# Second half of a weight load cut in two, and the last store handed to two queues, in a fused attention + gated-MLP kernel

## The chip, the core and the metric

The kernel runs on one core of a Trainium2 chip. A core has a matrix engine (TensorE, PE in the profile; its weight loads are listed as PEld), a vector engine (VectorE, DVE), a scalar engine (ScalarE, ACT), GpSimd (POOL) and SyncE (SP), which here only issues DMAs. Each engine runs its own list of instructions in order; they wait for one another through counters (semaphores). The metric is device time of the whole program in microseconds, the median of several runs; lower is better. The profiler also records one execution in full: its span runs from the first to the last recorded instruction.

## What is computed

The input is one sequence of 2048 tokens with 512 features. With LN for a layer norm without scale and bias, cut to what matters:

```python
xn = LN(A_x)                                  # 2048 x 512
# A: 32 heads of 16, each token looks at 8 keys, 2 tokens apart, backwards
q, k, v = split(xn @ A_wqkv)
a = softmax(q . k[s - 2w], w = 0..7) ; A = (sum_w a_w v[s - 2w]) @ A_wo
# B: gated MLP with mixing over tokens
z = gelu(xn @ B_w_in)                         # 2048 x 1376, halves z1 and z2
g = B_w_sp @ LN(z2) + B_b_sp                  # mixes over tokens
B = (z1 * g) @ B_w_out
out = A_x + A + B                             # 2048 x 512, bfloat16
```

## The kernel before

The 2048 tokens are 16 tiles of 128 tokens (`P`). The order of the work is written out by hand: every engine runs its instructions in the order in which the program names them, so moving a line moves the work in that engine's list.

The start is what the first edit touches. SP issues the loads in this order: tile 0 of x, tile 1 of x (lines 180 and 181), tiles 2 and 3 together (182), then the z2 half of `B_w_in` into `w_z2` (lines 183 and 184), then the next four tiles of x (`load_x`, line 176), the two weights for q and k (188) and two more loads of x. `w_z2` holds 128 partitions by 4 row blocks (`kc` = 0 to 3, 128 of the 512 features each) by 688 columns. Before, it comes in two loads of two row blocks each. VectorE takes the layer-norm statistics of a tile (`ln_stats`), ScalarE the square root (`roots`), VectorE the reciprocal and the normalized tile `xn` (`ln_apply`). For the first four tiles PE transposes `xn` in four blocks into a PSUM tile `pt` (`transpose_pe`, line 224), and ScalarE (tiles 0 and 1, line 226) or VectorE (tiles 2 and 3, line 228) copies it into `xnT`. Before the first real work PE runs small matmuls on a tile of ones (`spin`, line 102).

`z2_part(i, pz, kc)` (line 239) is the product of tile i with row block kc: two matmuls of 344 columns each (line 241), accumulated in PSUM over the four values of kc. `z2_gelu` (line 245) is ScalarE's gelu of the finished tile. Lines 439 to 452 interleave tiles 0 and 1: block 0 and 1 of both, then blocks 2 and 3 of tile 0 with its gelu, then the transposes of tile 2, then blocks 2 and 3 of tile 1 with its gelu, then the transposes of tile 3, then `z2_tile(2)` and `z2_tile(3)` whole.

In between lie the products for q, k and v, the sliding attention on VectorE, the mixing over tokens (line 576, the largest single part of PE's work), z1 (588) and the output products (747 and 756). These are not touched.

The end is what the second edit touches. `out_b` and `store` (lines 742 and 760) finish one tile of 128 tokens after another: six matmuls, one add on VectorE, and one store of 128 KB from SP (764). The very last tile is finished by `last_tile` (line 722) in two halves of 256 columns: six matmuls (729), an add on VectorE (731) and a store of 64 KB (732), both stores issued from SP. After that the program ends (the records at line 809): SP waits until every completion counter has its count, and all engines meet.

Each DMA adds 16 to a completion counter when it has landed. The trace shows eight such counters (numbers 100, 102, 104, 105, 106, 107, 109, 110), which the DMAs of SP and ACT take in turn in program order, so that a DMA waits for the one that used its counter eight DMAs earlier. GpSimd's DMAs have counters of their own (111 to 115).

Of the kernel before, what the change touches and what calls it, by code (L numbers as in the profile page):

```python
# [13 lines left out]
P = 128  # L14
# [16 lines left out]
F = 1376  # L31
FH = 688
# [15 lines left out]
def kernel(  # L48
# [17 lines left out]
    A = nc.scalar  # L66
    G = nc.gpsimd
    PE = nc.tensor
    SP = nc.sync

    x2 = A_x.rearrange("b s d -> (b s) d")
    out2 = out.rearrange("b s d -> (b s) d")
# [14 lines left out]
    def bank_pair(name, two=False):  # L87
        turn[0] += 1
        pool = ps_b if turn[0] % 3 == 0 and not two else ps_a
        return pool.tile([P, 2, 512], F32, name=name, tag="mm")  # L90
# [66 lines left out]
    w_z2 = e1.tile([P, C, FH], BF16, name="w_z2")  # L157
# [11 lines left out]
    w_in_r = B_w_in.rearrange("(k p) f -> p k f", p=P)  # L169
# [10 lines left out]
    SP.dma_start(x0[:, 0, :], x2[0:P, :])  # L180
    SP.dma_start(x0[:, 1, :], x2[P:2 * P, :])
    SP.dma_start(x0[:, 2:4, :], x2[2 * P:4 * P, :].rearrange("(i p) d -> p i d", p=P))  # L182
    for k0 in (0, 2):
        SP.dma_start(w_z2[:, k0:k0 + 2, :], w_in_r[:, k0:k0 + 2, FH:F])
    xq.append(x0)
    load_x(1)
    for s in range(2):
# [12 lines left out]
    def ln_apply(i):  # L200
        xn = xnp.tile([P, D], BF16, name="xn")
        V.tensor_scalar(xn[:], xq[i // 4][:, i % 4, :], mv[:, i, 0:1], rstd[:, i:i + 1], ALU.subtract, ALU.mult)
        return xn
# [17 lines left out]
    def transpose_pe(i, xn):  # L221
        pt = ps_aux.tile([P, C, P], BF16, name="pt", tag="aux")
        for c in range(C):
            PE.transpose(pt[:, c, :], xn[:, c * P:(c + 1) * P], ident[:])  # L224
        if i < 2:
            A.copy(xnT[:, :, i * P:(i + 1) * P], pt[:])  # L226
        else:
            V.tensor_copy(xnT[:, :, i * P:(i + 1) * P], pt[:])
# [10 lines left out]
    def z2_part(i, pz, kc):  # L239
        for hh in range(2):  # L240
            PE.matmul(pz[:, hh, 0:FHALF], xnT[:, kc, i * P:(i + 1) * P],  # L241
                      w_z2[:, kc, hh * FHALF:(hh + 1) * FHALF],
                      start=(kc == 0), stop=(kc == C - 1))

    def z2_gelu(i, pz):

        kw = dict(accum_out=zsum[:, i:i + 1]) if i not in ZV else {}
        A.activation(z2[:, i, :].rearrange("p (a b) -> p a b", a=2), pz[:, :, 0:FHALF],  # L248
                     ACT.Gelu_apprx_tanh, **kw)
# [187 lines left out]
    roots(3, 4)  # L437

    pz = [bank_pair("pzb") for _ in range(2)]
    for kc, i in ((0, 0), (1, 0), (0, 1), (1, 1), (2, 0), (3, 0)):  # L440
        z2_part(i, pz[i], kc)
    z2_gelu(0, pz[0])
    xn2 = ln_apply(2)
    recip(3)
    xn3 = ln_apply(3)
    transpose_pe(2, xn2)
    z2_part(1, pz[1], 2)
    z2_part(1, pz[1], 3)
    z2_gelu(1, pz[1])
    transpose_pe(3, xn3)  # L450
    z2_tile(2)
    z2_tile(3)
# [269 lines left out]
    def last_tile(i, rest):  # L722

        ot = otp.tile([P, D], BF16, name="ot")
        for q, n0, n1 in ((SP, 0, 256), (SP, 256, 512)):
            ns = slice(n0, n1)
            po = ps_o[0].tile([P, D], F32, name="po")
            for m in range(MCH):
                PE.matmul(po[:, ns], uT[:, m, i * P:(i + 1) * P], wout[:, m, ns],  # L729
                          start=(m == 0), stop=(m == MCH - 1))  # L730
            V.tensor_tensor(ot[:, ns], po[:, ns], rest[:, ns], ALU.add)
            q.dma_start(out2[i * P:(i + 1) * P, ns], ot[:, ns])

# [43 lines left out]
    for jj in range(2, 4):  # L779
        for k in range(NG):  # L780
            if (jj, k) == (3, NG - 1):
                last_tile(tokens_of(jj, k), rest)
            else:
                out_b(jj, k, False)
                store(jj, k)
# [28 lines left out]
```

## Time and profile before

| | us |
|---|---|
| time, median of 3 runs | 201.28 (200.75 to 201.32) |
| time of the profiled execution | 200.6 |
| its span | 198.9 |
| PE busy | 194.0 (98% of the span) |
| DVE busy | 178.5 (90%) |
| ACT busy | 105.1 (53%) |
| POOL busy | 18.5 (9%) |
| granted TensorE clock, share of full speed | 1.000 |
| first real matmul (line 241) starts | 6.50 |
| last add on VectorE (line 731) starts | 195.96 |

The profiled execution is one run: its 200.6 us are 198.9 us of span and 1.7 us around it. Durations below are read from it. A line of the profile names the line of the program, the engine, the operation, and then what it writes and reads; buffer numbers are left out, so that `w_z` stands for `w_z1` and `w_z2`.

### The profile page before, as it was taken

The page shows a single profiled execution, that of the slowest core. Times are in us where ns is not written, and L with a number is a line of the kernel's source. Part 1 is how long each engine was busy: PE and PEld are TensorE (multiplying, and loading weights), DVE is VectorE, ACT ScalarE, POOL GpSimd, SP SyncE. Part 2 cuts the span into 40 slices and gives each one's busy share as a digit, 9 for nine tenths or more (in the row PEclk, how much of TensorE's full clock was granted, in tenths as well). Part 3 has the DMA queues.
Part 4 walks back from the last instruction along what each step waited for, and adds up shares of the span by engine and source line. Part 5 has one row for each costly group of instructions (what it writes and reads, how often), then busy time and mean ns, then how long its engine had stood idle before and what let it go on. Part 6 is the DMA issues. An engine that isn't in the chain of part 4 may idle for free.

```text
span 198.9 us, 3852 instructions
## 1 busy us (share of the span) xinstructions
PE 194.0 (98%) x1558; PEld 119.9 (60%) x1564; DVE 178.5 (90%) x208; ACT 105.1 (53%) x151; POOL 18.5 (9%) x65
## 2 busy tenths in 40 slices
PE   7999999999999999999999999999999999999994
PEld 7655655556666666666566666666666664444442
DVE  4799979999999999999999999999999999974083
ACT  4768987768898999486531277494133330000000
POOL 3036540002220020200100000000000000000000
PEclk9999999999999999999999999999999999999999
DMA  5984845999999239999899999799655132015733
GB/s 161 342 276 81 170 78 99 163 261 174 183 188 191 47 30 201 206 214 169 191 211 157 272 179 208 133 220 191 110 146 145 37 59 44 5 42 145 270 110 101
DMA packets 68770, 30.86 MB, mean 155 GB/s; under 512 B 57248, under 2 KB 67344, under 8 KB 68624
## 3 DMA queue, kind: packets, MB, share of 16 engines
q1 hardware_dynamic: 66976, 25.24, 59.4%
q0 software_dynamic: 1360, 5.24, 14.3%
q8 instruction: 12, 0.20, 0.4%
q10 hardware_dynamic: 416, 0.14, 0.3%
q14 instruction: 6, 0.05, 0.1%
HBM read 9.79 MB, written 2.10 MB: 60 GB/s over the span
## 4 chain that ended last, share of the span: by engine, by line
PE 92%; DMA 4%; DVE 1%; SPq 1%; issue 1%
PE pg L576 38%; PE pq L291 10%; PE po L747 10%; PE pzb L241 10%; PE pz L588 9%; PE pv L316 7%; PE pq L303 3%; PE po L756 3%; DMA out_dram<-ot 2%; DMA w_z<-in_B_w_in_dram 2%; PE pl L363 1%; DVE ot L763 1%; PE po L729 1%; PE pt L224 0%; SPq L182 0%
## 5 line engine op out<-in xcount | busy, mean ns | idle before, releaser
L576 PE MATMUL pg<-z,wspT 128*128 128x344 bf16 x512 | 77.1, 310 | 0.0
L576 PEld LDWEIGHTS <-wspT 128*128 128x128 bf16 x512 | 50.0, 98 | 25.0 <-issue 0.4
L657 DVE TENSOR_TENSOR pw<-vp,a_sb 128x4096 bf16<-128x4096 bf16 x16 | 36.2, 2286 | 0.1
L579 ACT ACTIVATE gs<-pg,b_col 128x688 bf16<-128x688 f32 x16 | 13.3, 832 | 38.4 <-PE pg L576 38.4
L344 DVE TENSOR_TENSOR pr<-qk 128x8192 bf16<-128x8192 bf16 (+1 forms) x8 | 30.9, 3879 | 0.0
L588 PE MATMUL pz<-w_z,xnT 128*128 128x344 bf16 x128 | 21.3, 310 | 0.0
L241 PE MATMUL pzb<-w_z,xnT 128*128 128x344 bf16 x128 | 19.9, 309 | 0.3 <-DMA w_z<-in_B_w_in_dram 0.3
L747 PE MATMUL po<-wout,uT 128*128 128x512 bf16 x88 | 19.3, 379 | 0.2 <-DMA out_dram<-ot 0.2
L662 DVE TENSOR_TENSOR pw<-pw 128x4096 bf16<-128x4096 bf16 x8 | 18.3, 2288 | 0.1
L241 PEld LDWEIGHTS <-xnT 128*128 128x128 bf16 x128 | 12.4, 98 | 6.9 <-ACT xnT L226 0.3
L588 PEld LDWEIGHTS <-xnT 128*128 128x128 bf16 x128 | 12.4, 98 | 6.3 <-issue 0.3
L294 ACT CAST qk<-pq 128x1024 bf16<-128x1024 f32 x12 | 12.1, 1012 | 5.8 <-PE pq L291 5.8
L351 DVE TENSOR_TENSOR pr<-pr 128x2048 bf16<-128x2048 bf16 (+1 forms) x10 | 15.1, 1535 | 0.1
L747 PEld LDWEIGHTS <-uT 128*128 128x128 bf16 x90 | 8.7, 98 | 10.7 <-issue 0.4
L316 PE MATMUL pv<-xnT,wv 128*32 128x512 bf16 x256 | 14.4, 380 | 0.0
L592 ACT ACTIVATE z1b<-pz 128x688 bf16<-128x688 f32 x16 | 11.9, 743 | 4.0 <-PE pz L588 3.9
L248 ACT ACTIVATE z<-pzb 128x688 bf16<-128x688 f32 x16 | 11.8, 740 | 2.0 <-PE pzb L241 1.9
L291 PE MATMUL pq<-xnT,wk 128*128 128x512 bf16 x47 | 12.3, 379 | 0.1
L756 PE MATMUL po<-wo_r,op 32*128 32x512 bf16 x224 | 12.3, 375 | 0.0
L316 PEld LDWEIGHTS <-wv 128*32 128x32 bf16 x256 | 9.5, 139 | 4.5 <-issue 0.3
L291 PE MATMUL pq<-xnT,wq 128*128 128x512 bf16 x46 | 12.1, 380 | 0.1
L763 DVE TENSOR_TENSOR ot<-po,xr 128x512 bf16<-128x512 f32 x15 | 9.4, 684 | 2.9 <-PE po L756 1.8
(101 smaller groups left out, 201.6 us busy)
## 6 DMA issues: line engine op xcount, KB each, us to landing
pr<-pr POOLq DMA_DIRECT2D x4, 1024.0 KB, 10.1
xr<-in_A_x_dram SPq DMA_DIRECT2D x4, 512.0 KB, 4.6
out_dram<-ot SPq DMA_DIRECT2D x15, 128.0 KB, 1.8
wo_r<-in_A_wo_dram SPq DMA_DIRECT2D x4, 448.0 KB, 4.8
xq<-in_A_x_dram SPq DMA_DIRECT2D x2, 512.0 KB, 7.5
qk<-qk POOLq DMA_DIRECT2D x1, 1024.0 KB, 11.3
w_z<-in_B_w_in_dram SPq DMA_DIRECT2D x2, 344.0 KB, 4.7
w_z<-in_B_w_in_dram SPq DMA_DIRECT2D x1, 688.0 KB, 5.3
```

Of the source, the lines that this page charges most:

```text
L241: PE.matmul(pz[:, hh, 0:FHALF], xnT[:, kc, i * P:(i + 1) * P], w_z2[:, kc, hh * FHALF:(hh + 1) * FHALF], start=(kc == 0), stop=(kc == C - 1))
L291: PE.matmul(pq[:, s, :], wqk_v[s][:, kc, c], xnT[:, kc, tsl], start=(kc == 0), stop=(kc == C - 1))
L316: PE.matmul(pv[32 * k:32 * k + 32, dd, :].rearrange("p (b t) -> p b t", b=NB), wv_v[:, kc, 2 * d2 + dd, :], xnT_g[:, kc, :, k, :], start=( ...
L344: V.tensor_tensor(pr[:, :, cs, :], qk[hb][:, cs, 0, HALO:HALO + SB].unsqueeze(1).broadcast_to([P, 2, n, SB]), shifted(qk[hb][:, cs, 1, off ...
L351: V.tensor_tensor(pr[:, :, 0:n, :], pr[:, :, 0:n, :], pr[:, :, n:2 * n, :], ALU.add)
L576: PE.matmul(pg[:, hh, 0:FHALF], wsps[j][:, k, :], z2[:, k, hh * FHALF:(hh + 1) * FHALF], start=(k == 0), stop=(k == NT - 1))
L579: A.activation(gs[:], pg[:, :, 0:FHALF], ACT.Identity, bias=b_col[:, j:j + 1])
L588: PE.matmul(pz[:, hh, 0:FHALF], xnT[:, kc, j * P:(j + 1) * P], w_z1[:, kc, hh * FHALF:(hh + 1) * FHALF], start=(kc == 0), stop=(kc == C - 1))
L657: V.tensor_tensor(pw[:], shifted(vp[:, :, hb, off:off + P]), a_sb[:, 2 * p:2 * p + 2, osl].unsqueeze(2).broadcast_to([P, 2, DH, P]), ALU.mult)
L662: V.tensor_tensor(pws[p - 1][:], pws[p - 1][:], pw[:], ALU.add)
L747: PE.matmul(pos[jj, k][:], uT[:, m, i * P:(i + 1) * P], wout[:, m, :], start=first and m == 0, stop=not first and m == MCH - 1)
L756: PE.matmul(pos[jj, k][:], op[32 * k:32 * k + 32, d, jj * P:(jj + 1) * P], wo_r[32 * k:32 * k + 32, d, :], start=first and d == 0, stop=(n ...
```

## The change

The second load of `w_z2` becomes two loads of one row block each, so that SP issues one DMA more ahead of the next tiles of x. PE's order at the start becomes: blocks 0 and 1 of tiles 0 and 1, block 2 of both, the transposes of tile 2, then block 3 of tile 0 and its gelu, block 3 of tile 1 and its gelu, then the transposes of tile 3. In `last_tile` the store of the second half of the columns is cut by partitions: SP stores partitions 0 to 63, ScalarE's queue partitions 64 to 127.

```diff
-    for k0 in (0, 2):
-        SP.dma_start(w_z2[:, k0:k0 + 2, :], w_in_r[:, k0:k0 + 2, FH:F])
+    for k0, k1 in ((0, 2), (2, 3), (3, 4)):
+        SP.dma_start(w_z2[:, k0:k1, :], w_in_r[:, k0:k1, FH:F])
...
-    for kc, i in ((0, 0), (1, 0), (0, 1), (1, 1), (2, 0), (3, 0)):
+    for kc, i in ((0, 0), (1, 0), (0, 1), (1, 1), (2, 0), (2, 1)):
         z2_part(i, pz[i], kc)
-    z2_gelu(0, pz[0])
     xn2 = ln_apply(2)
     recip(3)
     xn3 = ln_apply(3)
     transpose_pe(2, xn2)
-    z2_part(1, pz[1], 2)
-    z2_part(1, pz[1], 3)
-    z2_gelu(1, pz[1])
+    for i in range(2):
+        z2_part(i, pz[i], 3)
+        z2_gelu(i, pz[i])
     transpose_pe(3, xn3)
...
-        for q, n0, n1 in ((SP, 0, 256), (SP, 256, 512)):
+        for n0, n1 in ((0, 256), (256, 512)):
...
-            q.dma_start(out2[i * P:(i + 1) * P, ns], ot[:, ns])
+            for q, p0 in ((SP, 0), (A, 64)) if n0 else ((SP, 0),):
+                p1 = 64 if n0 and not p0 else P
+                q.dma_start(out2[i * P + p0:i * P + p1, ns], ot[p0:p1, ns])
```

## Prediction

> **What bounds the kernel now.** I read the busy times first, then the chain that ended last in order of time, then the timelines of its two ends. The first row:
>
> ```profile
> PE 194.0 (98%) x1558; PEld 119.9 (60%) x1564; DVE 178.5 (90%) x208; ACT 105.1 (53%) x151; POOL 18.5 (9%) x65
> ```
>
> PE is busy nearly throughout. The chain in order of time (start, duration, what) shows how the two ends hang on it:
>
> ```profile
> 2.19 4.27 DMA w_z<-in_B_w_in_dram
> 6.46 0.04 issue
> 6.50 2.04 PE pzb L241 x12
> 8.54 0.22 PE pt L224 x4
> 8.76 0.58 PE pzb L241 x4
> 9.34 0.22 PE pt L224 x4
> 9.57 2.33 PE pzb L241 x16
> ...
> 29.21 1.17 PE pzb L241 x8
> ...
> 194.62 1.32 PE po L729 x12
> 195.94 0.02 issue
> 195.96 0.42 DVE ot L731
> ```
>
> The first load of w_z2 lets PE start at 6.50. From there I went through PE's matmul starts one by one. Apart from single missing records there is one hole, at the ninth matmul, and after it PE never waits again up to 195.9. So what PE gains after 6.50 reaches the end, and so does what is added after 195.96. The hole on PE's timeline, matmuls and then weight loads:
>
> ```profile
> 6.50 2.04 PE L241 MATMUL pzb<-w_z,xnT 128*128 128x344 bf16 x12 [0.33 <-DMA w_z<-in_B_w_in_dram]
> ```
>
> ```profile
> 7.79 0.39 PEld L241 LDWEIGHTS <-xnT 128*128 128x128 bf16 x3 [0.17 <-issue]
> ```
>
> Eight such matmuls take 1.17 us in the chain, 0.146 each. Twelve, the last to its end (0.31), should take 11 x 0.146 + 0.31 = 1.92; the row has 2.04. The difference stands at one place: the eighth starts at 7.52, the ninth at 7.80 instead of 7.67. That ninth is row block 2 of tile 0 and waits for the counter of the second w_z2 load, whose sixteenth part landed at 7.754 (issued at 2.705, 5.05 us). **The hole is 0.13 us.**
>
> **Loads and order at the start.** The second load (344 KB) becomes two of 172 KB. Consecutive loads of this queue land in order: the first ends at 6.462, the second at 7.754, the next x at 9.233. Between the first two lie 1.29 us for 344 KB, so block 2 should be there near 6.462 + 0.65 = 7.1 and block 3 near 7.75 as before.
>
> In the new order eight matmuls run from 6.50 to 7.67, and block 2 of both tiles from 7.67 to 8.25, covered by a load 0.55 us ahead. The four transposes of tile 2 (0.22) need `xn` of tile 2, ready at 7.57: to 8.47. Block 3 of both tiles runs to 9.05, its load there 0.7 us earlier, then the transposes of tile 3 to 9.28; tile 2 starts there instead of at 9.41. The count of matmuls and transposes is the same, so the gain is the hole: **-0.13 us**. It can't be more in this execution, since PE has no other wait there; if block 2 doesn't land before the whole did, it is 0.
>
> What is late next: VectorE's copy of tile 2 (0.42) moves forward with the transposes, keeping its lead of about 0.13 over tile 2's matmuls. Tile 0's gelu is ready near 8.96 instead of 8.92; its table load ended at 8.90 anyway. Its PSUM pair is wanted at 10.44 and free near 9.8.
>
> The extra issue is one DMA on SP. Issues there come 0.51 apart, so x tiles 4 to 7, both q/k weights and the last two x loads are issued 0.51 later. They hide behind the backlog:
>
> ```profile
> xq<-in_A_x_dram SPq DMA_DIRECT2D x1, 512.0 KB, 6.0
> ```
>
> This x load is issued at 3.22 and lands 6.0 us later although it is the next to move; the queue, not the issue, sets the landing, and the bytes are the same. VectorE wants it at 9.82 (landed 9.23), PE wants wq at 11.46 (landed 10.72). Without that cover the issue could cost up to 0.51 minus these leads, nothing still. I take 0.
>
> **The last store.** The two half-tile stores on SP's timeline, and the DMA view of the second alone (64 KB, us to landing):
>
> ```profile
> 195.80 0.95 SPq L732 DMA_DIRECT2D out_dram<-ot  x2
> ```
>
> ```profile
> out_dram<-ot SPq DMA_DIRECT2D x1, 64.0 KB, 1.5
> ```
>
> In detail: the add ends at 196.39, SP issues from 196.418 for 0.332, the last part lands at 197.949, 1.53 after issue. The first half's issue ended at 196.184, so SP's queue stood empty when the second became due; a second queue saves no waiting for SP. The data packets fill only 197.25 to 197.59, on the same 16 DMA engines whichever queue they come from.
>
> No row shows a 64-partition store from ACT. Bounds: half the rows in each queue could take half of the 0.35 us of packets away, at best -0.17. From the other side there are ACT's small transfers (32 partitions, 16 KB):
>
> ```profile
> L646 ACTq DMA_DIRECT2D uT<-op x8: 514/600/1182, 175.1 to 180.4; - x8
> ```
>
> Here 514/600/1182 are the least, middle and greatest ns of an issue. They land 1.78 to 1.88 after issue, three of the eight later (2.40, 2.71, 3.17). But SP's issues of the same transfer, alone, also take 0.58 and land at 1.76 to 1.84, so the length belongs to that transfer more than to ACT. SP's full stores, 1.70 alone, take 1.81 to 2.13 beside ACT's, +0.11 to +0.43. The nearest row is the same store from SP (1.53), and beside another queue its smallest surcharge: **+0.10 us**, range -0.17 to +0.43.
>
> On such splits the Trainium skill ("DMA: Bandwidth & Descriptors", rules for kernel authors) speaks against the change: two transfers to disjoint partition halves are not worth making, because both go over all 16 engines and serialize. The packets above agree that the engines are shared; by that rule alone the term would be 0 and the sum 0.10 lower.
>
> **The closing waits.** This isn't in the diff. After its last issue SP goes through all completion counters in fixed instructions, seen in the trace's semaphore records (start us, counters):
>
> ```
> 196.796 [100]        196.855 [102] [115]   196.921 [104] [114]
> 196.986 [105] [113]  197.047 [106] [112]   197.106 [107] [111]
> 197.420 [109] [101]  197.966 [110] [108]   198.033 drain
> ```
>
> A satisfied wait costs 0.062 (five steps from 196.796 to 197.106). Now the last store is on the last counter in the list, 110: nothing is left behind it but the drain. SP's and ACT's DMAs take the eight counters in turn. One more load at the start and one more store at the end shift this: the last full store goes from 107 to 109, the first half to 110, SP's quarter to **100** and ACT's to **102**. If SP walks the list in the same order, it stands at 100 and 102 until 197.95, and then has six satisfied waits, 104 to 110, still before it: 6 x 0.062 = **+0.37 us** (seven, 0.43, if 100 lands last). The rotation changes nothing else: in the middle each DMA still waits for the eighth before it, and at the start for loads landed by 5.5.
>
> Is the list by number or by age? Here the two agree for SP's counters. Against age: POOL's counters, used last at 47 to 80 us, stand beside the younger ones and run newest first. I take number.
>
> **Sum**, against the profiled execution: 200.6 - 0.13 + 0 + 0.10 + 0.37 = 200.94, +0.34. That run lies 0.68 under the median shown; carried to the median, 201.28 + 0.34 = 201.62, +0.17%. A measurement of this kernel can tell about 0.3% (0.60 us) from no change.
>
> **Rivals.**
> - *The list goes by age* (18%). The last store then stays last in the list, with at most one wait (0.06) more: -0.13 + 0.10 + 0.06 = +0.03, about 201.3; with the store at -0.17, 201.0. For it: the shown list is also in order of age. Against it: POOL's counters.
> - *The queues hold one another up*, ending slower (20%). Both quarters become due in the same instant. ACT's issue at 177.03, beside SP's store at 177.13, took 1.18 and landed at 2.40, 0.87 over 1.53; SP's store went to 2.13, +0.43. With 0.24 from the other two terms this gives +0.67 to +1.11, 201.95 to 202.4. It decides from the point where a quarter lands over 1.89 after its issue (0.24 + 0.36 = 0.60). For it: three of ACT's eight rows. Against it: those lay among 12 other transfers, the last store is alone.
> - *The split load does not help* (7%): block 2 lands no sooner than the whole, as it would if the slowest of the 16 engines set both ends. Then -0.13 is 0 and the sum +0.47, 201.75. Against it: the slowest parts are also 1.29 apart per 344 KB.
> - *The hole is larger outside the profiled run* (7%). The runs shown spread by 0.57, all above the 200.6; if late landings of the second load make 0.5 of that, the gain is 0.6 and the sum -0.1 to -0.2, 201.1, and with the list by age 200.7.
>
> **How the numbers follow.** The forecast has the remaining 48%, 201.3 to 202.0 by the store's bounds. The range 200.9 to 202.1 holds it, both small cases, most of age and the lower third of the queues' case. Faster by over 0.3% needs large hole and age together with a good store: 7%. Slower needs 0.60: the queues' case (20%) and the upper edge of the forecast's store: 23%. The rest, 70%, is within 0.3%.
>
> **What would show it.** Right: the w_z row of 12 matmuls at 1.92 and transposes at 8.25; tile 2 at 9.28; PE's last matmul 0.13 earlier; SP's closing list with [100] and [102] waiting till the last landing and six records 0.062 apart behind them. Wrong: 110 again last in the list (age), a quarter landing over 1.89 after issue (queues), a second hole in PE before 12 us, or a wait of line 303 for wq (the extra issue not covered).

## The result, and the profile after

| | before | after |
|---|---|---|
| time, median of 21 runs each | 200.76 us | 201.43 us |
| ratio after/before | | 1.0033 (95%: 1.0017 to 1.0049) |
| span of the profiled execution | 198.9 | 199.6 |
| first matmul of line 241 | 6.504 | 6.347 |
| ninth (block 2 of tile 0) | 7.796 | 7.525 |
| first load of w_z2 landed | 6.462 | 5.777 |
| ScalarE's first copy into `xnT` (line 226) ends | 6.225 | 6.291 |
| last add on VectorE ends | 196.391 | 196.121 |
| from there to the span's end | 2.466 | 3.489 |

The changed kernel is slower by 0.33%, 0.67 us, and in the profiled pair this lies entirely in the last 3.5 us. Up to the last add everything is 0.27 us earlier; behind it 1.02 us are added. 1.02 - 0.27 = 0.75 is the difference of the two spans.

The start, on PE's timeline of the profile after (start, duration, instructions; before, the first row was 2.04 long and had a wait in front of it):

```profile
6.34 1.92 PE L241 MATMUL pzb<-w_z,xnT 128*128 128x344 bf16 x12
8.10 0.39 PE L224 MATMUL pt<-ident,xn 128*128 128x128 bf16 x4
```

The twelve matmuls now take the 1.92 us that twelve without a hole should take, and no wait for a load of w_z2 is shown ahead of them. The chain after shows what sets their start now (start, duration, what); before, the first load of w_z2 stood in this place:

```profile
4.80 0.42 DVE xn L202
5.22 0.05 issue
5.27 0.41 PE pt L224 x4
5.68 0.02 issue
5.70 0.59 ACT xnT L226
6.30 0.05 issue
6.34 1.92 PE pzb L241 x12
```

PE waits for ScalarE's copy of tile 0, and the load has been there for 0.5 us. The busy row is the same work as before:

```profile
PE 193.6 (97%) x1558; PEld 119.6 (60%) x1564; DVE 178.6 (89%) x208; ACT 105.1 (53%) x151; POOL 18.5 (9%) x65
```

The end, on the timeline after:

```profile
195.53 1.16 SPq L733 DMA_DIRECT2D out_dram<-ot  x2
195.69 0.42 DVE L730 TENSOR_TENSOR ot<-po,rest 128x256 bf16<-128x256 f32 x1 [0.23 <-PE po L728]
196.15 0.56 ACTq L733 DMA_DIRECT2D out_dram<-ot  x1
```

and in the DMA view of the last two issues (KB, us from issue to landing):

```profile
out_dram<-ot SPq DMA_DIRECT2D x1, 32.0 KB, 1.9
out_dram<-ot ACTq DMA_DIRECT2D x1, 32.0 KB, 2.1
```

Each queue carries half of what SP carried in 1.5 us before, and each takes longer: SP's part 1.86, ACT's 2.12. SP's wait view has the program's last line waiting for them (it was 0.8 in two waits before):

```profile
SPq L810 <- DMA out_dram<-ot: 1.6, 1, 1.6
```

SP's closing semaphore records of the profile after show what stands behind this wait. ACT's part is on counter 100, SP's on 102:

```
198.289 [100]        198.347 [102] [115]   198.414 [104] [114]
198.478 [105] [113]  198.539 [106] [112]   198.599 [107] [111]
198.660 [109] [101]  198.719 [110] [108]   198.787 drain
```

ACT's part landed at 198.272; the drain, which stood 0.067 behind the record of the last store before, stands 0.498 behind it now.

### The profile page after: what moved, and what is told of

It reads as the page before. It is cut to its first block, busy times and chain, and to the rows that moved or that the text cites. A ratio compares the mean times of both kernels' runs of the same rounds, so it can differ in the third digit from the quotient of the medians.

```text
span 199.6 us, 3856 instructions
## 1 busy us (share of the span) xinstructions
PE 193.6 (97%) x1558; PEld 119.6 (60%) x1564; DVE 178.6 (89%) x208; ACT 105.1 (53%) x151; POOL 18.5 (9%) x65
## 4 chain that ended last, share of the span: by engine, by line
PE 92%; DMA 3%; DVE 2%; issue 1%; ACT 0%
PE pg L575 37%; PE pq L291 10%; PE po L748 10%; PE pzb L241 9%; PE pz L587 9%; PE pv L316 7%; PE pq L303 3%; PE po L757 3%; DMA out_dram<-ot 2%; DMA xq<-in_A_x_dram 1%; PE pl L363 1%; PE po L728 1%; DVE stats L197 1%; DVE ot L764 1%; PE pt L224 0%
```

## The experiments

All start from the kernel before. Where a comparison needs the number of DMAs to come out right, small loads are added in the middle of the token mixing, with n of them:

```diff
-    late1.tile([P, HALO * C * 2], BF16, name="gap")
+    gap = late1.tile([P, HALO * C * 2], BF16, name="gap")
...
+        if j == 10:
+            for e in range(n):
+                SP.dma_start(gap[0:NT, 16 * e:16 * e + 16], B_b_sp.rearrange("(j p) -> j p", p=P)[:, 0:16])
```

Two numbers are given for each. The time is compared with runs of the kernel before on the same chip. The ratio and its interval are worked out from the single runs and are not the quotient of the two medians printed beside them; a few tenths of a microsecond can lie between the two, and where they differ the ratio counts. A kernel with a single execution has no ratio. The **tail**, from the end of the last add to the end of the span, comes from one profile; it is 2.466 before. Four kernels whose last stores were left alone and on counter 110 (eight_more, start_seven, order_alone, split_load_seven) came within 0.03 of it.

### The closing list

> The kernel before with one small load more (512 bytes into an unused tile, issued by SP in the middle of the token mixing, where SP is idle); the start and the last store are as before. Theory of the closing list: the last store moves from counter 110 to counter 100, seven satisfied waits of 0.062 us stand behind its landing, +0.43 us, and the semaphore records show [100] waiting for the last landing. Rival (the whole loss lies in the split store, the closing list is free): 0.

The small loads above, n = 1. Measured 200.89 against 200.50, ratio 1.0020 (1.0000 to 1.0040); tail 2.865, +0.40. The store itself is as before (landed 1.523 after issue), and its landing is waited for at the head of the list:

```
197.658 [100]        197.716 [102] [115]   197.783 [104] [114]
197.847 [105] [113]  197.909 [106] [112]   197.968 [107] [111]
198.029 [109] [101]  198.089 [110] [108]   198.156 drain
```

In this profile one 512-byte load 60 us before the end costs 0.4 us at the end. The timed ratio says the same size, with an interval that just touches 1; start_alone below shows the same tail again.

> As one_more, but with eight small loads. Theory of the closing list: the rotation comes round, the last store is on 110 again, 0 us. Rival (each further DMA costs time, about 0.05 us by what one_more would then show): +0.4 us.

n = 8. Measured 200.56 against 200.50, ratio 1.0003 (0.9983 to 1.0023); tail 2.457. Eight loads cost nothing where one cost 0.4: it is the place in the list that counts, not the load. The list goes by number, not by age.

### The start

> The edit at the start alone (load of blocks 2 and 3 in two, new order on PE), the last store as before, and seven small loads so that the last store is on counter 110 again. Theory (the start gains on average what the profiled pair shows): 0.13 to 0.27 us faster than before, PE's first matmul of line 241 runs without a hole. Rival (the earlier start in the profile after was chance, only the hole of 0.13 goes, and in many runs there is none): 0 to 0.13 faster.

The load and order edits of the change, the last store as before, n = 7. Measured 200.36 against 200.50, ratio 0.9987 (0.9972 to 1.0002); tail 2.470, no hole. The ratio (-0.26 us) and the medians (-0.14) agree with the theory, but the interval still holds 1.

> The edit at the start alone, the last store as before, no small loads: one load more than before, so the last store is on counter 100. Theory (terms add): -0.14 from the start and +0.39 to +0.43 from the closing list, 0.25 to 0.3 us slower than before, although everything up to the last add is earlier. Rival (the closing list does not matter on average): 0.14 faster.

The same without the small loads. Measured 200.95 against 200.72, ratio 1.0018 (1.0003 to 1.0032); tail 2.871. The interval, +0.06 to +0.64 us, holds the theory's sum and leaves out the rival. The closing list's share is in the tail, +0.40. An earlier start is not in this profile: its first matmul starts at 6.55 and its last add ends at 196.58, both later than before, because PE was still at about half rate there (last section).

> Only PE's new order (block 2 of both tiles, transposes of tile 2, block 3 of both tiles); the loads and the last store as before. Theory (the order is not what gains): first load of w_z2 landed at 6.2 to 6.5, PE's first matmul of line 241 at 6.3 to 6.5, time within 0.1 us of before. Rival (the order gains the 0.14): 0.1 to 0.2 faster.

Only the second part of the diff. Measured 200.44 against 200.72, ratio 1.0009 (0.9991 to 1.0027), so no difference is shown; here the medians point the other way, by 0.28 us. The first load of w_z2 landed at 5.70 and the first matmul started at 6.33: the landing is earlier than the theory said, with the loads uncut.

> Only the load of blocks 2 and 3 cut in two, PE's order and the last store as before, seven small loads so that the last store is on 110. Theory (the cut of the second load lets the first one land earlier, as in after and start_seven): first load landed at 5.7 to 5.8 instead of 6.2 to 6.5, no hole at the ninth matmul, 0.1 to 0.2 us faster than before. Rival (the early landing was chance): landed at 6.2 or later and no gain.

Only the first part of the diff, and n = 7. Measured 200.26 against 200.72, ratio 0.9983 (0.9965 to 1.0001); first load landed at 5.79, no hole. The nearest of all to a gain, but not clear of 1 either.

The profiles together say more on the start than any one. In nine with the second load whole, the first load landed between 5.70 and 6.80 (middle 6.21) and a hole at the ninth matmul stood in two (0.13, and 0.28 in sp_twice_seven below). In five with it cut, it landed between 5.64 and 5.90 (middle 5.78), with no hole in any. An early landing is worth little by itself: ScalarE's copy of tile 0 ends between 6.23 and 6.49 in all fourteen, and the first matmul reads what it writes. In all five with the cut, and in five of the nine without, that copy sets the first matmul, 0.05 us after its end; in eight_more copy and load tie. Only in before, store_seven and act_whole does PE wait for the load alone, for 0.04 to 0.51 us beyond the copy.

### The last store

> The split of the last store alone, the start as before, and seven small loads so that the two parts are on the last two counters again. Theory (the two queues hold one another up): the later part lands about 2.1 us after its issue as in the profile after, 0.59 later than before's 1.53, and the time is 0.6 longer. Rival (the late landing was chance, the loss is the closing list): the part lands at 1.5 to 1.7, 0 to 0.15 longer.

The third part of the diff, and n = 7. Measured 201.15 against 200.50, ratio 1.0029 (1.0012 to 1.0046); tail 3.074, +0.61. SP's part landed 1.84 after issue, ACT's 2.10: the late landing is no chance. The next runs take it apart.

> The kernel before, with the last store cut to partitions 0 to 63 from SP; the other 64 tokens' second half of the columns is left out and never stored. Theory (the two queues hold one another up, each is fast alone): issue 0.33, last part landed at most 1.53 us after issue. Rival (a store of 64 partitions is slow in itself, with nothing beside it): issue 0.54 and landed at 1.84 to 1.86, as SP's part in store_seven and after.

```diff
-            q.dma_start(out2[i * P:(i + 1) * P, ns], ot[:, ns])
+            p1 = 64 if n0 else P
+            SP.dma_start(out2[i * P:i * P + p1, ns], ot[0:p1, ns])
```

One execution: 200.77, tail 2.787, +0.32. The half store, from SP with nothing beside it, in the instruction view of out_dram (least, middle, greatest ns of an issue; the least is the first half-tile with all 128 partitions) and in the DMA view:

```profile
L733 SPq DMA_DIRECT2D out_dram<-ot x2: 384/462/539, 195.7 to 196.3; - x2
```

```profile
out_dram<-ot SPq DMA_DIRECT2D x1, 32.0 KB, 1.9
```

Half the bytes, and the issue is 0.539 instead of 0.332, the landing 1.85 instead of 1.53. The loss stands ahead of the data: the first packet comes 1.19 after the start of the issue (0.83 before), while the packets take 0.31 (0.35 before). My theory of two queues that hold one another up falls for this part: the store of 64 partitions is slow in itself.

> The kernel before, with the whole last store (128 partitions, 64 KB) issued by ACT instead of SP. Theory (ACT's queue is no slower, the loss is the cut into two): issue 0.33 to 0.36, landed at about 1.53, time as before. Rival (ACT's queue is slower, as its part in after, 0.565 and 2.12, suggests): issue about 0.56, landed at 1.8 or later, 0.25 or more longer.

```diff
-        for q, n0, n1 in ((SP, 0, 256), (SP, 256, 512)):
+        for q, n0, n1 in ((SP, 0, 256), (A, 256, 512)):
```

Measured 200.61 against 200.64, ratio 1.0012 (0.9990 to 1.0033); tail 2.498. In the same two views:

```profile
L732 ACTq DMA_DIRECT2D out_dram<-ot x1: 377/377/377, 196.6 to 196.6; - x1
```

```profile
out_dram<-ot ACTq DMA_DIRECT2D x1, 64.0 KB, 1.6
```

With all 128 partitions ACT lands in 1.583, 0.05 after SP's 1.531. ACT's queue by itself is not the cause.

> The last store cut in two halves of 64 partitions, both issued by SP one after the other, and seven small loads so that the second is on counter 110. Theory (each half is slow in itself and they go one after the other, whatever the queue): the first half lands 1.84 after its issue, the second's issue follows 0.6 later, and it lands about 2.4 after the first's issue, 0.3 later than ACT's half in after. Rival (only two queues at once are slow): the second lands by 0.33 + 1.53 = 1.9 after the first's issue.

```diff
+            for q, p0 in ((SP, 0), (SP, 64)) if n0 else ((SP, 0),):
```

in place of the pair (SP, 0), (A, 64), n = 7. One execution: 201.49, tail 3.416, +0.95. The first part landed 1.84 after its issue, the second, issued 0.59 later, 2.48 after the first's issue. Both halves are slow, and one queue pays for them in turn.

> The last store handed to two queues by columns instead of partitions: SP stores columns 256 to 383 and ACT columns 384 to 511 of all 128 partitions, 32 KB each, the start as before, seven small loads so that both are on the last two counters. Theory (two separate causes: stores of 64 partitions are slow in themselves, and transfers of two queues that start together go one after the other): issues back to 0.33 to 0.38, SP's part lands at about 1.5, ACT's data packets begin where SP's end, about 0.25 later, and it lands at about 1.8, 0.2 to 0.3 us longer than before. Rival (only the 64 partitions are slow, two queues run side by side): both land at 1.55 or earlier, 0 to 0.1 faster than before.

```diff
+            for q, c0, c1 in ((SP, 256, 384), (A, 384, 512)) if n0 else ((SP, 0, 256),):
+                q.dma_start(out2[i * P:(i + 1) * P, c0:c1], ot[:, c0:c1])
```

n = 7. Measured 200.83 against 200.51, ratio 1.0027 (1.0006 to 1.0047); tail 2.624, +0.16, the smallest tail of the three ways to cut the store. The timed ratio, +0.54 us with an interval of 0.12 to 0.94, does not separate it from store_seven.

```profile
out_dram<-ot SPq DMA_DIRECT2D x1, 32.0 KB, 1.5
out_dram<-ot ACTq DMA_DIRECT2D x1, 32.0 KB, 1.6
```

With all partitions the issues are 0.332 and 0.383, and the landings 1.47 and 1.63. ACT's packets start at 197.107, 0.12 after SP's first (196.986) and before SP's last (197.265). So the strict "one after the other" of my theory was too strong here; in the profile after, with 64 partitions, SP's packets start between 197.338 and 197.618 and ACT's between 197.607 and 197.892. In both the second queue is the later one, by 0.12 and by 0.27.

### The whole change with the list put right

> The changed kernel whole with six small loads in the middle, so that the parts of the last store are on counters 109 and 110. Theory (three terms that add: start -0.14, closing list +0.43, store +0.59 to +0.65): the closing list's 0.43 goes, 0.4 us faster than the changed kernel, 0.45 to 0.5 slower than before. Rival (the closing waits only hide something that comes up elsewhere): as the changed kernel, 0.67 slower than before.

The whole diff, and n = 6. Measured 201.02 against 200.64, ratio 1.0020 (1.0006 to 1.0034); tail 3.113. Against the changed kernel's tail of 3.489 the closing list's share is gone (0.38); the split store's 0.65 stays.

## Why the prediction was right, and where it was off

The forecast was 0.34 us slower, the runs show 0.67 (0.34 to 0.98 by the interval). That the time itself came so near, 201.43 for a forecast 201.62, is luck: 201.62 stands on a median of three runs, 201.28, which 21 runs put at 200.76, and from there the same sum gives 201.10. The 0.33% lies just over the 0.3% from which the prediction spoke of slower, which it gave 23%. Its four terms beside what the runs showed:

| term | forecast | shown |
|---|---|---|
| start | -0.13 | -0.27 in the profiled pair; -0.26 by start_seven's ratio, interval -0.56 to +0.04 |
| extra issue on SP | 0 | 0: no wait for x or wq appears on PE, the x load behind landed at 9.32 (9.23 before) |
| last store | +0.10 | +0.59 in the profile, +0.61 in store_seven's tail |
| closing list | +0.37 | +0.43 in the profile, +0.40 in one_more's tail |

In the profiled pair the misses are -0.14 at the start, +0.49 at the store and +0.06 in the list. Their sum, +0.41, leads from 0.34 to the 0.75 between the spans. The signs are right in every term; the size of the whole was half.

**The closing list** was right in mechanism and nearly in size. ACT's part took counter 100 and landed last, so seven satisfied waits stood behind it rather than six. The rival that the list goes by age is out by one_more and eight_more.

**The start** was right for the hole: it is gone in every kernel with the cut load. That the gain "can't be more" than the hole held only with the first matmul fixed at 6.50. It started 0.16 earlier in the profile after, since the first load landed at 5.78 instead of 6.46. More was not to be had there: ScalarE's copy, which the prediction does not look at, holds PE until 6.29 in that profile, and held it until 6.23 before. Block 2 landed at 7.35, not near 7.1, and lay 0.18 ahead of its matmul where 0.55 was expected; it was enough.

Five profiles against nine point the same way, yet their ranges overlap and no timed run of the start is clear of 1. Whether the cut of the second load brings the first forward is left open. The profile of before was also not typical: seven of nine profiles with the load whole have no hole. The term of 0.13 was worked out from one execution's late landing. The rival of a larger hole outside the profiled run is not supported, the holes seen are 0.13 and 0.28; what came late by more is the first load, by 0.51 in act_whole. (That rival's last figure, 200.7 with the list by age, comes to 200.8 by its own terms.)

**The last store** is the mis-sized term, 0.10 for 0.59. The step that failed is "The nearest row is the same store from SP (1.53)". The step before it, "the length belongs to that transfer more than to ACT", was true (act_whole lost 0.05), but the conclusion drawn from it was wrong. The 32-partition transfers, with 0.58 of issue and 1.76 to 1.84 to landing on SP alone, shared with the new store that they use only part of the partitions; I set them aside as the wrong form and took the 128-partition store as the nearest row. sp_half_only shows it: 0.539 and 1.85 at 64 partitions, 0.32 more than the whole store, and SP's first part of 64 partitions landed at 1.84 to 1.86 in the four other profiles that have one. The other 0.26 is ACT's part coming behind SP's. By act_whole 0.05 of it may be ACT's queue; no run stores 64 partitions from ACT alone. The two together, 2.12 after issue, lie beyond the 1.89 from which the rival of the two queues was to decide. Its price (0.43 to 0.87) held the truth; its mechanism, that the queues slow one another, explains at most the 0.26.

What makes this store of 64 partitions slower to issue than one of 128 is not shown. With 128 partitions of half as many columns (columns_seven) the issue is back at 0.332, so it is not the size of the transfer. Nor is it the number of partitions alone: in the profile before, two loads of 32 partitions (line 709) issue in 0.41 each, and four more (line 713) in 0.32 to 0.57.

On the split by partitions the Trainium skill ("DMA: Bandwidth & Descriptors", rules for kernel authors) said not to bother, because the halves serialize. The packet times above agree that ACT's part comes behind SP's. The page names no price; read as a loss of nothing, as the prediction read it, the rule is too mild, since the split cost 0.59 us here.

The terms add in the tails: 0.40 (one_more) + 0.61 (store_seven) = 1.01, against 1.02 in the changed kernel. The timed ratios add as well, with wide intervals: -0.26 (start_seven) + 0.40 (one_more) + 0.58 (store_seven) = 0.72 against 0.66.

No version beats the kernel before beyond doubt. The start edits with the last store left whole and on counter 110 come out at 0.9987 and 0.9983 of it, both intervals touching 1.

## What to carry to other kernels

Count what the program does after its last landing, and where the last DMA stands in it: here one DMA more, in the middle (one_more) or at the start (start_alone), moved the end by 0.4 us, which is more than the edit at the start gained in the profiles. Don't cut the last small transfer without measuring it: the packets are 0.35 us of this store's 1.53, and a store of half the partitions was slower than the whole one. Before bringing a load forward, ask what else its reader waits for: here it was a copy that ended 0.24 us before the load landed. When an operation has no row of its own, ask what it shares with each near row before dropping one: here it was the use of part of the partitions, and not the queue, that the new store shared with the slow rows.

## What the runs showed of the hardware that was not expected

- A store of 64 partitions by 512 bytes takes 0.539 us to issue and 1.85 to land, one of 128 partitions by 512 bytes 0.332 and 1.53, both from SP with nothing beside them.
- Issued 4 to 5 ns apart by SP and ACT, two stores don't start together: the second queue's first packet came 0.12 us (128 partitions) and 0.27 us (64 partitions) after the first's.
- In two of the fourteen profiles, eight_more and start_alone, PE's opening ran at about half rate until about 7 us: their first two steps between matmuls of 344 columns are 0.26 to 0.29 us instead of 0.146. The trace's record of the granted clock, at full speed, begins at 6.91 and 7.11 us there, just where the steps become short, and at 4.04 to 6.00 in the other twelve. The window view prints 1.00 also for the stretch ahead of that record, so that the view alone hides the slow opening. The Trainium skill ("TensorE: Matmul & The Clock Gate", Part 1) puts the change to the full rate down to a window of activity that runs free of the kernel's start, so that it comes at a different place from run to run. The profiles agree with a varying place; and the full-speed record is 191.15 us long in these two and 194.56 in the others, a difference of 3.41 us, which is the length that the page gives for the window. It is one source of the spread at the start, in which gains of 0.1 us are hard to tell.
